# One operand of a VectorE product is read from PSUM instead of SBUF in a decode attention kernel

## The chip, the cores and the metric

The kernel runs on one core of one Trainium2 chip. The metric is device time in microseconds (us). Three runs of the kernel before took 1329.06, 1330.38 and 1332.26 us; the median is 1330.38 us. One further execution was recorded with the hardware profiler; every duration below is from it.

The engines are named as the profile names them: PE (TensorE, matrix products; PEld is its weight load), DVE (VectorE), ACT (ScalarE), POOL (GpSimd) and SP (SyncE, which here only starts transfers). SBUF is the working memory, PSUM the memory that PE writes its products to.

## What is computed

One decoding step of a transformer block with four sequences, one new token each:

```python
def _A_ref(x, k_cache, v_cache, wq, wo):          # B=4, Sq=1, D=512, H=32, Sk=4096, Dh=128
    q = (x @ wq).reshape(B, Sq, H, Dh).transpose(0, 2, 1, 3)
    scores = jnp.einsum("bhqd,bhkd->bhqk", q, k_cache) * (Dh ** -0.5)
    p = _softmax(scores, axis=-1)
    o = jnp.einsum("bhqk,bhkd->bhqd", p, v_cache)
    return o.transpose(0, 2, 1, 3).reshape(B, Sq, H * Dh) @ wo

mod = (_silu(c) @ w_mod).reshape(c.shape[0], 6, 1, -1)
sa, ca, ga, sb, cb, gb = (mod[:, i] for i in range(6))
h = _layernorm(x) * (1 + ca) + sa
x = x + ga * _A_ref(h, A_k_cache, A_v_cache, A_wq, A_wo)
h = _layernorm(x) * (1 + cb) + sb
x = x + gb * (_silu(h @ w1) @ w2)                 # F=1792
```

All arrays are float32. The two caches hold 4 x 32 x 4096 x 128 numbers each, 268 MB apiece, and every one of them is read once. The remaining inputs are weights of 1 to 8 MB.

## The kernel before

**Tiles.** The attention is cut into 32 tiles. A tile `n` is one sequence `b` and a group of four heads. Its keys are 8.39 MB (4 heads x 4096 x 128 x 4 bytes); its values are as many. A tile's keys lie in SBUF as 128 partitions by 128 rows of 128 numbers: partition `32*i + p` belongs to head `i` of the four.

**Buffers.** Three areas of 64 KB per partition, A, B and C. The keys alternate between B (even tiles) and A (odd tiles). There is one area, C, for the values.

**Order of the transfers.** All large transfers are started by SP from one queue, in the order of the program: the keys of tile n+1, then (after tile n) the values of tile n+1, then the keys of tile n+2, and so on. SP waits in front of a transfer until the area it overwrites has been read for the last time. So the values of n+1 are started when PE has finished the last product with the values of n; the keys of n+2, behind them in the queue, when tile n's keys have been read, which is earlier.

**One tile** (`tile`, then `values`):

- The keys are multiplied by the query in place: DVE takes the first 48 rows (its query operand lies in PSUM, banks 0 and 1, where `qload` puts it), POOL takes rows 48 to 128 in three instructions (48 to 80, 80 to 104, 104 to 128) with the query in SBUF.
- DVE sums each row (`scores`, `TENSOR_REDUCE sc<-k`): rows 0 to 48, then 48 to 80.
- For the first 80 rows DVE finds the maximum, ACT takes the exponentials, and `spread(0, 80)` writes `pz`: each exponential times a mask of four columns that is 1 for the partition's own head and 0 for the other three. This is 320 numbers per partition.
- DVE sums rows 80 to 104 and 104 to 128, and the same follows for these 48 rows: maximum, exponentials, `spread(80, 128)` with 192 numbers per partition.
- PE multiplies `pz` into the values (`pv`), first for rows 0 to 80 into bank 2, then for the rest into bank 3. The quotient by the sum of the exponentials and the merge of the two halves follow on DVE, ACT and PE.

The mask is `mask`, a tile of 128 x 4 numbers in SBUF, which DVE computes once at the start from the identity matrix.

```python
def spread(lo, hi):
    g0, g1 = lo // JJ, hi // JJ
    w = pz[:, g0:g1, :, :]
    tt("DVE", w, bc(ev[:, g0:g1, :], 2, HP), bc(bc(mask[:, :], 1, g1 - g0), 3, JJ))
```

`bc` repeats an operand along a dimension without copying it, so the mask's four columns are read again and again.

**Ahead of the loop** the modulation, the first layer norm and the queries are computed; PE uses bank 7 there for parts of the modulation and of the queries. **Behind the loop** the output weights `wot` (area B, four transfers) and the weights of the feed-forward part `w1t` (three transfers) and `w2t` (five transfers, both in area A) follow in SP's queue. PE projects the attention's output with `wot` into columns 0 to 127 of bank 7 (`project`), and the feed-forward part ends the program. The last tile's keys and values come in two transfers each (rows 0 to 80 and 80 to 128).

The order of the work on every engine is the order of the program. Waits are derived from which regions an operation reads and writes; in PSUM a region is a whole bank, within a quarter of the partitions.

Of the kernel before, what the change touches and what calls it, by code (L numbers as in the profile page):

```python
# [6 lines left out]
AF = mybir.ActivationFunctionType  # L7
# [177 lines left out]
def build(nc, x, kc, vc, wq, wo, w1, w2, c, wm, out):  # L185
    P = 128
# [3 lines left out]
    G = 4  # L190
    W = P // G
    HP = 4
# [4 lines left out]
    JJ = 4  # L197
# [13 lines left out]
    def sb(name, *shape, at=None):  # L211
        size = 4
        for s in shape:
            size *= s
        if at is None:
            at = base[0]
            base[0] += -(-size // 32) * 32
            assert base[0] <= nc.sbuf_usable_end, (name, base[0])
        return nc.alloc_sbuf_tensor_at(name, [P, *shape], F32, offset=at)
# [10 lines left out]
    bank = [nc.alloc_psum_tensor(f"ps{i}", [P, 512], F32) for i in range(8)]  # L230
    dsem = {}

    def dma(dst, src, tag, eng="SP"):
        if tag not in dsem:
            dsem[tag] = nc.alloc_semaphore("d_" + tag)
        s = dsem[tag]
        e = pl.eng[eng]
        return pl.op(eng, lambda: e.dma_start(dst, src), [], [dst], sem=s)  # L238

    def dve(f, reads, writes):  # L240
        return pl.op("DVE", f, reads, writes)

    def act(f, reads, writes):
        return pl.op("ACT", f, reads, writes)
# [14 lines left out]
    def tt(eng, o, a, b, op=ALU.mult):  # L259
        e, q = (V, dve) if eng == "DVE" else (GP, pool)  # L260
        return q(lambda: e.tensor_tensor(o, a, b, op=op), [a, b], [o])  # L261
# [10 lines left out]
    def actv(o, a, fn, scale=1.0, bias=None, accum=None):  # L272
        kw = {"scale": scale}
        reads, writes = [a], [o]
        if not isinstance(scale, float):
            reads.append(scale)
        if bias is not None:
            kw["bias"] = bias
            if not isinstance(bias, float):
                reads.append(bias)  # L280
        if accum is not None:
            kw["accum_out"] = accum
            writes.append(accum)
        return act(lambda: A.activation(o, a, fn, **kw), reads, writes)  # L284

    def bc(a, dim, n):
        a = a.unsqueeze(dim)
        shape = list(a.shape)
        shape[dim] = n
        return a.to_broadcast(shape)  # L290
# [4 lines left out]
    mask = sb("mask", G)  # L295
# [71 lines left out]
    def vload(n, *cuts):  # L367
        t, b = divmod(n, B)
        src = vc[b, HP * t : HP * (t + 1)].rearrange("h (p j) d -> (h p) j d", p=W)
        cuts = cuts or (0, NJ)  # L370
        for i, (lo, hi) in enumerate(zip(cuts, cuts[1:])):
            tag = "C" if len(cuts) == 2 else f"v{i}"
            dma(vt[:, lo:hi, :], src[:, lo:hi, :], tag)
# [83 lines left out]
    def qexpand(t):  # L457
        j, g = divmod(t, G)
        ps = bank[2 + t % 2]
        for i in range(HP):  # L460
            mm(
                ps[W * i : W * (i + 1), :], mask[:, g : g + 1].to_broadcast([P, W]),
                E[:, HP * j + i, :, :].rearrange("p b d -> p (b d)"), True, True,
            )
        actv(qw[:, t, :], ps[:, :], AF.Copy)
# [10 lines left out]
    for t in range(1, NT):  # L476
        qexpand(t)
    vload(0)
    for i in (2, 3):
        dve(lambda i=i: V.memset(bank[i][:, :], 0.0), [], [bank[i][:, :]])  # L480

    ev = ea.rearrange("p (g j) -> p g j", j=JJ)
# [7 lines left out]
    def spread(lo, hi):  # L490
        g0, g1 = lo // JJ, hi // JJ
        w = pz[:, g0:g1, :, :]
        tt("DVE", w, bc(ev[:, g0:g1, :], 2, HP), bc(bc(mask[:, :], 1, g1 - g0), 3, JJ))

    def ownmax(h, src, col):
        rm = sc[:, col : col + 1]
# [16 lines left out]
    def tile(n):  # L513
        t, b = divmod(n, B)
        k = kt[n % 2]
        tt("DVE", k[:, :ND, :], k[:, :ND, :], bc(bank[n % 2][:, :Dh], 1, ND))
        for lo, hi in zip(CUTS, CUTS[1:]):
            tt("POOL", k[:, lo:hi, :], k[:, lo:hi, :], bc(qview(n), 1, hi - lo))
        scores(n, (0, ND))
        scores(n, (ND, NA))  # L520
        ownmax(0, sc[:, :NA], NJ)
        actv(ea[:, :NA], sc[:, :NA], AF.Exp, bias=nm[:, 0:1], accum=rs[:, 0:1])
        spread(0, NA)
        for lo, hi in zip(CUTS[1:], CUTS[2:]):
            scores(n, (lo, hi))
        ownmax(1, sc[:, NA : NJ + 1], NJ + 1)
        actv(ea[:, NA:], sc[:, NA:NJ], AF.Exp, bias=nm[:, 1:2], accum=rs[:, 1:2])
        actv(X[:, 1:2], nm[:, 0:1], AF.Exp, scale=-1.0, bias=nm[:, 1:2])
        spread(NA, NJ)
        stt(X[:, 0:1], rs[:, 0:1], X[:, 1:2], rs[:, 1:2], ALU.mult, ALU.add)  # L530
        if n + 1 < N:
            qload(n + 1)
# [130 lines left out]
```

## Time and profile before

| | |
|---|---|
| median of three runs | 1330.38 us |
| profiled execution | 1325.98 us, of which the span from the first to the last instruction is 1324.6 us |
| DVE busy | 984.4 us, 74% of the span |
| POOL busy | 710.3 us, 54% |
| PE busy | 402.1 us, 30% |
| ACT busy | 83.8 us, 6% |
| read from HBM | 567.30 MB, 428 GB/s over the span |
| mean granted PE clock | 0.65 |

In the views of the profile a row of the timeline gives the start, the duration, the engine, the line of the code, the operation with its output and inputs, and in brackets how long the engine had stood idle before it and for what. A row of groups gives the busy time of all such instructions, the mean of one, and the idle time before them. A row of windows gives a stretch, its length, the busy time of each engine in it with the number of instructions, and at its end the granted PE clock, the share in which the 16 DMA engines were busy, and the rate of the transfers.

### The profile page before, as it was taken

How to read it: one execution, taken by the hardware profiler on the slowest of the kernel's cores; microseconds unless marked ns; L12 is line 12 of the kernel's file. 1: busy time of each engine (PE TensorE's matmuls, PEld its weight loads, DVE VectorE, ACT ScalarE, POOL GpSimd, SP SyncE). 2: the span in 40 equal slices, each digit the busy share in tenths (PEclk: the TensorE clock that was granted, in tenths of full speed). 3: DMA queues.
4: the chain of work that ended last, by engine and by line, in shares of the span. 5: the costliest groups of instructions: out<-in, count | busy, mean ns of one | idle time of the engine just before them, and what ended most of it. 6: DMA issues, size and time to landing. Idle time of an engine off the chain costs nothing.

```text
span 1324.6 us, 7211 instructions
## 1 busy us (share of the span) xinstructions
PE 402.1 (30%) x3032; PEld 122.9 (9%) x3032; DVE 984.4 (74%) x582; ACT 83.8 (6%) x289; POOL 710.3 (54%) x104
## 2 busy tenths in 40 slices
PE   2433212333311333322133332223333212333346
PEld 1100000000000000000000000000000000000014
DVE  1378877777887777788777778777778877777881
ACT  1200000000000000000000000000000000000001
POOL 0345665444666544566644456655445665444750
PEclk9766566666556666655666665566666566666577
DMA  9999999999999999999999999999999999999998
GB/s 412 442 414 439 440 424 434 418 440 422 438 437 432 429 432 426 440 433 434 433 426 435 436 434 430 433 428 431 434 424 438 433 424 436 432 431 430 424 423 344
DMA packets 12125, 567.78 MB, mean 429 GB/s; under 512 B 1292, under 2 KB 1340, under 8 KB 2108
## 3 DMA queue, kind: packets, MB, share of 16 engines
q1 hardware_dynamic: 12052, 567.29, 99.4%
q8 instruction: 24, 0.39, 0.1%
q14 instruction: 9, 0.07, 0.0%
q10 hardware_dynamic: 40, 0.02, 0.0%
HBM read 567.30 MB, written 0.01 MB: 428 GB/s over the span
## 4 chain that ended last, share of the span: by engine, by line
DMA 55%; DVE 36%; PE 6%; ACT 1%; issue 1%; SPq 1%; POOL 0%; another core or an unknown queue 0%
DMA k<-in_A_k_cache_dram 49%; DVE sc L270 22%; DVE k L261 8%; PE ps L252 6%; DVE pz L261 5%; DMA wot<-in_A_wo_dram 3%; DMA wqt<-in_A_wq_dram 3%; ACT sc L284 1%; DVE rt L499 1%; SPq L238 1%; DVE nm L269 0%; POOL E L261 0%; DVE hidT L402 0%; DVE hid L265 0%
## 5 line engine op out<-in xcount | busy, mean ns | idle before, releaser
L261 POOL TENSOR_TENSOR k<-k,qw 128x3072 f32<-128x3072 f32 (+1 forms) x96 | 705.8, 7380 | 521.6 <-DMA k<-in_A_k_cache_dram 521.6
L252 PE MATMUL ps<-v,pz 128*16 128x512 f32 x2048 | 312.1, 752 | 854.0 <-DVE pz L261 854.0
L270 DVE TENSOR_REDUCE sc<-k 128x24 f32<-128x3072 f32 (+2 forms) x128 | 559.3, 4409 | 1.1
L261 DVE TENSOR_TENSOR k<-k,ps 128x6144 f32<-128x6144 f32 x32 | 209.7, 6554 | 126.1 <-DMA k<-in_A_k_cache_dram 126.1
L252 PEld LDWEIGHTS ps<-v,pz 128*16 128x16 f32 x2048 | 57.7, 113 | 1051.3 <-DVE pz L261 887.4
L261 DVE TENSOR_TENSOR pz<-sc,mask 128x320 f32<-128x320 f32 x64 | 127.6, 1994 | 32.5 <-ACT sc L284 32.5
L284 ACT ACTIVATE sc<-sc,nm 128x80 f32<-128x80 f32 x64 | 22.3, 348 | 1015.4 <-DVE nm L269 1015.4
L265 DVE SCALAR_TENSOR_TENSOR o<-ps,fr,o 128x512 f32<-128x512 f32 x32 | 24.0, 750 | 52.7 <-PE ps L252 52.7
L252 PE MATMUL ps<-sel,o 128*128 128x4 f32 x256 | 33.8, 255 | 27.9 <-DVE o L265 27.9
L538 DVE RECIPROCAL fr<-ps 128x1 f32<-128x1 f32 x32 | 5.4, 168 | 42.5 <-PE ps L252 42.5
L252 PEld LDWEIGHTS ps<-sel,o 128*128 128x128 f32 x256 | 31.0, 191 | 59.9 <-DVE o L265 59.9
L261 POOL TENSOR_TENSOR E<-qs,sel 128x2048 f32<-128x2048 f32 x1 | 3.6, 3640 | 45.5 <-ACT qs L284 45.5
L284 ACT ACTIVATE o<-ps,fr 128x512 f32<-128x512 f32 x32 | 22.0, 687 | 60.8 <-DVE fr L265 60.8
L270 DVE TENSOR_REDUCE sc<-sc 128x1 f32<-128x80 f32 x64 | 14.1, 220 | 2.2
L499 DVE STREAM_TRANSPOSE rt<-sc 128x32 f32<-128x32 f32 x64 | 13.5, 212 | 2.2
L252 PE MATMUL ps<-wmt,csT 128*32 128x256 f32 (+1 forms) x64 | 8.3, 697 | 18.2 <-DMA wmt<-in_w_mod_dram 18.2
L284 ACT ACTIVATE oz<-ps 128x4 f32<-128x4 f32 (+2 forms) x40 | 7.4, 197 | 97.5 <-PE ps L252 97.5
L269 DVE TENSOR_REDUCE nm<-rt 128x1 f32<-128x32 f32 x64 | 11.9, 186 | 2.2
L261 DVE TENSOR_TENSOR E<-qs,sel 128x2048 f32<-128x2048 f32 x1 | 2.3, 2291 | 13.6 <-ACT qs L284 13.6
L252 PE MATMUL ps<-X,selp 128*128 128x2 f32 x64 | 12.3, 262 | 0.0
L252 PEld LDWEIGHTS ps<-X,selp 128*128 128x128 f32 x64 | 9.5, 188 | 27.3 <-DVE X L265 27.3
L284 ACT ACTIVATION_READ_ACCUMULATOR sc<-sc,nm 128x1 f32 x64 | 11.9, 186 | 0.0
(62 smaller groups left out, 121.2 us busy)
## 6 DMA issues: line engine op xcount, KB each, us to landing
wmt<-in_w_mod_dram SPq DMA_DIRECT2D x1, 6144.0 KB, 17.3
k<-in_A_k_cache_dram SPq DMA_DIRECT2D x1, 5120.0 KB, 35.9
v<-in_A_v_cache_dram SPq DMA_DIRECT2D x1, 5120.0 KB, 21.0
wot<-in_A_wo_dram SPq DMA_DIRECT2D x1, 4096.0 KB, 33.9
k<-in_A_k_cache_dram SPq DMA_DIRECT2D x1, 3072.0 KB, 42.8
v<-in_A_v_cache_dram SPq DMA_DIRECT2D x1, 3072.0 KB, 24.3
wot<-in_A_wo_dram SPq DMA_DIRECT2D x1, 2048.0 KB, 38.4
wot<-in_A_wo_dram SPq DMA_DIRECT2D x2, 1024.0 KB, 42.0
```

The costliest lines, as they stand in the source:

```text
L238: return pl.op(eng, lambda: e.dma_start(dst, src), [], [dst], sem=s)
L252: lambda: nc.tensor.matmul(o, lhsT, rhs, start=start, stop=stop, skip_group_check=True),
L261: return q(lambda: e.tensor_tensor(o, a, b, op=op), [a, b], [o])
L265: return dve(lambda: V.scalar_tensor_tensor(o, a, s, b, op0=op0, op1=op1), reads, [o])
L269: return dve(lambda: V.tensor_reduce(o, a, axis=AX.X, op=op, negate=True), [a], [o])
L270: return dve(lambda: V.tensor_reduce(o, a, axis=AX.X, op=op), [a], [o])
L284: return act(lambda: A.activation(o, a, fn, **kw), reads, writes)
L499: dve(lambda: V.transpose(rt[:, h, :], a), [rm], [rt[:, h, :]])
L538: dve(lambda: V.reciprocal(fr[:, 0:1], fps[:, 0:1]), [fps[:, 0:1]], [fr[:, 0:1]])
```

## The change

```diff
     for t in range(1, NT):
         qexpand(t)
     vload(0)
+    actv(bank[7][:, P : P + G], mask[:, :], AF.Copy)
     for i in (2, 3):
         dve(lambda i=i: V.memset(bank[i][:, :], 0.0), [], [bank[i][:, :]])
@@
     def spread(lo, hi):
         g0, g1 = lo // JJ, hi // JJ
         w = pz[:, g0:g1, :, :]
-        tt("DVE", w, bc(ev[:, g0:g1, :], 2, HP), bc(bc(mask[:, :], 1, g1 - g0), 3, JJ))
+        tt("DVE", w, bc(ev[:, g0:g1, :], 2, HP), bc(bc(bank[7][:, P : P + G], 1, g1 - g0), 3, JJ))
```

Ahead of the loop ACT copies the mask once into columns 128 to 131 of PSUM bank 7. Both spreads of every tile read it there. The numbers that are multiplied are the same. Nothing writes to bank 7 between this copy and `project`, behind the last tile, which writes its columns 0 to 127 when the last spread has been done.

ACT has one instruction more. It stands behind the last copy of an expanded query (`qw`), ahead of the load of the table for the exponentials and of the first tile's exponentials (`sc,rs<-sc,nm`):

```order
 L284 ACTIVATE ps<-qw 128x128
 L284 ACTIVATE qw<-ps 128x512 x7
+L284 ACTIVATE ps<-mask 128x4
 L284 ACT_TABLE_LOAD
 L284 ACTIVATE sc,rs<-sc,nm 128x80
```

Nothing behind it on ACT has another place. On DVE, in the first tile (`k_85` are its keys, `nm` the negative maximum, `pz` the spread exponentials), the changed kernel has:

```order
L269 TENSOR_REDUCE nm<-rt 128x1
L261 TENSOR_TENSOR pz<-sc,ps 128x320
L270 TENSOR_REDUCE sc<-k_85 128x24 x2
L270 TENSOR_REDUCE sc<-sc 128x1
L500 STREAM_TRANSPOSE rt<-sc 128x32
L269 TENSOR_REDUCE nm<-rt 128x1
L261 TENSOR_TENSOR pz<-sc,ps 128x192
```

The sequence is that of before; the two spreads name `ps` (PSUM) where they named `mask`. PE, POOL and SP have the same instructions in the same order.

## The prediction, made before the changed kernel had run

> **What bounds the kernel now.** The page comes first: the slices of the span, and the transfer queues.
>
> ```profile
> PE 402.1 (30%) x3032; PEld 122.9 (9%) x3032; DVE 984.4 (74%) x582; ACT 83.8 (6%) x289; POOL 710.3 (54%) x104
> DMA  9999999999999999999999999999999999999998
> GB/s 412 442 414 439 440 424 434 418 440 422 438 437 432 429 432 426 440 433 434 433 426 435 436 434 430 433 428 431 434 424 438 433 424 436 432 431 430 424 423 344
> q1 hardware_dynamic: 12052, 567.29, 99.4%
> DMA 55%; DVE 36%; PE 6%; ACT 1%; issue 1%; SPq 1%; POOL 0%; another core or an unknown queue 0%
> ```
>
> No compute engine is above 74%, while SP's one queue keeps the 16 DMA engines busy for 99.4% of the span and moves over 410 GB/s in every slice but the last. The last row is the chain of waits, and it seems to say something else: 36% of the span on DVE. So I look at one tile in the timeline, to see whether the transfers ever wait for DVE.
>
> ```profile
> 602.28 6.55 DVE L261 TENSOR_TENSOR k<-k,ps 128x6144 f32<-128x6144 f32 x1 [4.10 <-DMA k<-in_A_k_cache_dram]
> 602.33 22.05 POOL L261 TENSOR_TENSOR k<-k,qw 128x4096 f32<-128x4096 f32 x3 [16.65 <-DMA k<-in_A_k_cache_dram]
> 621.01 3.72 DVE L261 TENSOR_TENSOR pz<-sc,mask 128x320 f32<-128x320 f32 x1 [0.52 <-ACT sc L284]
> 624.65 6.60 DVE L270 TENSOR_REDUCE sc<-k 128x24 f32<-128x3072 f32 x2
> 624.78 6.19 PE L252 MATMUL ps<-v,pz 128*16 128x512 f32 x40 [25.49 <-DVE pz L261]
> 632.45 0.36 DVE L261 TENSOR_TENSOR pz<-sc,mask 128x192 f32<-128x192 f32 x1 [0.49 <-ACT sc L284]
> 636.13 0.33 SPq L238 DMA_DIRECT2D v<-in_A_v_cache_dram  x1
> 636.50 0.43 SPq L238 DMA_DIRECT2D k<-in_A_k_cache_dram  x1
> 640.98 6.55 DVE L261 TENSOR_TENSOR k<-k,ps 128x6144 f32<-128x6144 f32 x1 [4.09 <-DMA k<-in_A_k_cache_dram]
> ```
>
> Keys land at 602.28; 33.85 us later (636.13) PE is through with the values, and SP starts the next values and the next keys but one. The following keys, started a tile earlier, land only at 640.98. So when SP starts new transfers, 640.98 - 636.13 = 4.85 us of old ones are still under way. I call this the **cover**. The period is 640.98 - 602.28 = 38.70 us, and two transfers of 8.39 MB in it make 433.5 GB/s. The stretches by tile, and over the loop:
>
> ```profile
> 602.28:640.98 38.70, 10.45 (x74) 3.02 (x74) 30.48 (x17) 2.09 (x8) 22.05 (x3) 0.63 1.00 434
> 58.00:1224.60 1166.60, 330.83 (x2220) 92.03 (x2220) 914.36 (x510) 62.87 (x240) 661.66 (x90) 0.63 1.00 432
> ```
>
> The DMA share is 1.00 in both. **The transfers bound the loop.** DVE stands on the chain because SP starts the keys behind a wait for PE; a chain can't show that the transfer, once started, stands in line.
>
> **The change, part by part.** The groups with their shapes give the spread's price:
>
> ```profile
> L261 DVE TENSOR_TENSOR pz<-sc,mask 128x320 f32<-128x320 f32 x32 | 116.1, 3629 | 16.7 <-ACT sc L284 16.7
> L261 DVE TENSOR_TENSOR pz<-sc,mask 128x192 f32<-128x192 f32 x32 | 11.5, 359 | 15.8 <-ACT sc L284 15.8
> L261 DVE TENSOR_TENSOR E<-qs,sel 128x2048 f32<-128x2048 f32 x1 | 2.3, 2291 | 13.6 <-ACT qs L284 13.6
> L261 DVE TENSOR_TENSOR k<-k,ps 128x6144 f32<-128x6144 f32 x32 | 209.7, 6554 | 126.1 <-DMA k<-in_A_k_cache_dram 126.1
> ```
>
> The large spread takes ten times the small one, for 1.7 times the numbers. In the tile above POOL's three products end at 602.33 + 22.05 = 624.38, and the spread ends at 624.73, 0.35 us behind them. The small spread runs when POOL is idle. So DVE with two operands in SBUF stands still until POOL is done, whereas the keys' product, with one in PSUM, runs its 6554 ns beside POOL.
>
> *The spread's new time.* A line through the two rows that read SBUF alone and unhindered (192 numbers in 359 ns, 2048 in 2291) has 1.041 ns a number and 159 ns to begin with. It gives 492 ns for 320 numbers, and 6555 ns for 6144, where the row with a PSUM operand has 6554: PSUM costs nothing that shows. I take 0.49 us. Bounds: 0.36 us (the small spread) and 3.72 us (POOL still blocks it). [...]
>
> *What moves in a tile.* The large spread ends 3.72 - 0.49 = 3.23 us earlier, at 621.50. The next two sums take 6.60 us; the second starts near 624.8 and needs POOL's last product, done at 624.38, so it just finds it ready; if POOL were later, DVE would wait there. PE starts on `pz` at 621.6, is done with 40 products by 627.8, and the small spread is there at 632.45 + 0.36 - 3.23 = 629.58: PE still waits for DVE. So all that follows is 3.23 us earlier; SP starts the values at 632.90 instead of 636.13, and the cover becomes 8.08 us. DVE loses 32 x (3.63 - 0.49) = 100 us of busy time, 984 to 884, and its wait for the keys grows from 4.1 to 7.3 us a tile.
>
> *What the end gains:* nothing. A transfer started earlier stands longer in a line that is never empty. The same tile repeats, so loop: 0 of 1166.5 us.
>
> *ACT's copy of the mask*, once:
>
> ```profile
> L284 ACT ACTIVATE oz<-ps 128x4 f32<-128x4 f32 x32 | 5.7, 178 | 90.3 <-PE ps L252 90.3
> 55.29 1.28 ACT L284 ACT_TABLE_LOAD   x1
> 76.34 0.36 ACT L284 ACTIVATE sc<-sc,nm 128x80 f32<-128x80 f32 x1 [19.77 <-DVE nm L269]
> ```
>
> A copy of this size takes 178 ns (bounds 0 and the 0.60 us of a whole bank's copy). The table load behind it would end near 56.8 us, and ACT is next wanted at 76.34: the 19.77 us of idling hide it. Without them it would be 0.2 us, once. Both spreads wait for ACT's exponentials already, so no wait is added.
>
> *The last tile and the tail.*
>
> ```profile
> 1256.11 22.10 POOL L261 TENSOR_TENSOR k<-k,qw 128x4096 f32<-128x4096 f32 x3 [9.40 <-DMA k<-in_A_k_cache_dram]
> 1259.13 6.54 DVE L261 TENSOR_TENSOR k<-k,ps 128x6144 f32<-128x6144 f32 x1
> 1277.85 0.71 DVE L261 TENSOR_TENSOR pz<-sc,mask 128x320 f32<-128x320 f32 x1 [0.52 <-ACT sc L284]
> 1292.76 5.37 PE L252 MATMUL ps<-wot,oz 128*32 128x128 f32 x128 [0.93 <-DMA wot<-in_A_wo_dram]
> 1303.49 1.08 PE L252 MATMUL ps<-wot,oz 128*32 128x128 f32 x32 [1.51 <-DMA wot<-in_A_wo_dram]
> ```
>
> Here DVE comes to the keys late (POOL began at 1256.11, DVE at 1259.13), so it gains 3.0 us, and 0.2 us at the spread. But PE then waits for the weights at 1292.76 and again at 1303.49, both for DMA: the 3.2 us become waiting there. **Sum: 0 on 1325.98 us** (span 1324.6 and 1.4 around it). The profiled execution is 4.4 us below the median of the runs; a change of 0 leaves the median, **1330.4 us**.
>
> **The rivals.**
>
> *A: the cover was too small after all (faster).* The keys land 30 times between these rows:
>
> ```profile
> 58.10 6.56 DVE L261 TENSOR_TENSOR k<-k,ps 128x6144 f32<-128x6144 f32 x1 [2.16 <-DMA k<-in_A_k_cache_dram]
> 1224.60 6.55 DVE L261 TENSOR_TENSOR k<-k,ps 128x6144 f32<-128x6144 f32 x1 [4.10 <-DMA k<-in_A_k_cache_dram]
> ```
>
> That is 38.88 us a tile, 0.18 above the 38.70 of the tile shown; 30 x 0.18 = 5.5 us. If those were gaps because some of the 16 engines ran dry before SP's start, a cover of 8 us would close them: 1320.5, or 1324.9 by the runs. Against it stand the tiles in which PE was late:
>
> ```profile
> 870.52 0.33 SPq L238 DMA_DIRECT2D v<-in_A_v_cache_dram  x1
> 874.30 6.55 DVE L261 TENSOR_TENSOR k<-k,ps 128x6144 f32<-128x6144 f32 x1 [3.02 <-DMA k<-in_A_k_cache_dram]
> 912.86 6.55 DVE L261 TENSOR_TENSOR k<-k,ps 128x6144 f32<-128x6144 f32 x1 [3.95 <-DMA k<-in_A_k_cache_dram]
> ```
>
> The cover was 3.78 us there, and the next keys came 38.56 us later, no later than usual. Chance 0.10.
>
> *B: the DMA engines run further apart (slower).* A transfer has landed when the slowest of 16 engines has written its part. An engine that is ahead is now held at SP's start; with 3.23 us more in line it may get as far ahead again, and the slowest lags the mean by up to as much. It decides once engines differ by more than the old cover, 4.85 us, and costs once, not per tile, where the last `wot` lands: up to 3.2 us, 1329.2, or 1333.6 by the runs. For it: the intervals are not all equal (38.70, and 38.56 above). Against: every part of a transfer is of one size, and nothing in the rows shows engines apart. Chance 0.06.
>
> *C: the chain of waits is to be taken at its word (faster).* It passes DVE in every second tile: 16 x 3.23 = 52 us, 1274, or 1278 by the runs. Two tiles, 33.55 MB, would have to land in 77.40 - 3.23 = 74.17 us, 452 GB/s; the highest slice above is 442. [...] Chance 0.01.
>
> *D: the mask in PSUM doesn't free the spread.* It stays at 3.7 us; the time is the forecast's. Against it speaks the keys' product beside POOL. Chance 0.03.
>
> **How the numbers follow.** The forecast has 0.80. Its own range is the median with what three runs spread to either side and some more, 1327.9 to 1333.0. The range reaches towards A, down to where four fifths of the 5.5 us are gone (1326.0), and up to 1333.0; most of B and the far end of A are left out. A measurement of this kernel can tell about 0.2%, 2.7 us, from no change. Faster by more: A, C and 0.01 of the forecast's scatter, 0.12. Slower by more: B and 0.01 likewise, 0.07. Within: the rest with D, 0.81.
>
> **What would show it.** Right: the large spread near 0.5 us, DVE near 884 us busy, its wait for keys near 226 us in total (126.1 + 31 x 3.23), SP's start of the values 8 us before the keys land, keys still every 38.7 us, and in the tail longer waits of PE for `wot`. A is right if the intervals even out at 38.70; B if they, or the last `wot`, come later; D if the spread still ends with POOL. The forecast is wrong if the rate over the loop leaves 432 GB/s by more than 0.2% in either direction.

## The result, and the profile after

The changed kernel is faster: 1322.38 us (median of 4 runs, 1322.36 to 1322.80) against 1331.20 (4 runs, 1329.06 to 1332.26), a ratio of 0.9937 with a 95% interval of 0.9919 to 0.9954. In a second measurement of both (run g1 below) it was 1322.74 against 1328.46, ratio 0.9961 (0.9947 to 0.9976). That is 6 to 9 us, where the forecast was none. Two things stand out: the gain, and that the runs after lie within 0.4 us of each other where those of before spread over several. The profiled execution of before (1325.98) was faster than all four of its runs; the one after is 1322.36, with a span of 1321.0 us.

First the rows that the prediction named. The page of the changed kernel, engines, transfer queue and chain of waits:

```profile
PE 400.2 (30%) x3032; PEld 127.8 (10%) x3032; DVE 883.6 (67%) x582; ACT 83.9 (6%) x290; POOL 711.0 (54%) x104
q1 hardware_dynamic: 12052, 567.29, 99.5%
DMA 58%; DVE 34%; PE 6%; ACT 1%; issue 1%; SPq 0%; POOL 0%; another core or an unknown queue 0%
```

Its groups by shape (busy time in us, mean of one in ns, then the idle time ahead):

```profile
L261 DVE TENSOR_TENSOR k<-k,ps 128x6144 f32<-128x6144 f32 x32 | 209.7, 6554 | 218.9 <-DMA k<-in_A_k_cache_dram 218.9
L261 DVE TENSOR_TENSOR pz<-sc,ps 128x320 f32<-128x320 f32 x32 | 15.6, 487 | 16.7 <-ACT sc L284 16.7
L261 DVE TENSOR_TENSOR pz<-sc,ps 128x192 f32<-128x192 f32 x32 | 11.3, 354 | 15.8 <-ACT sc L284 15.8
```

The large spread takes 487 ns where it took 3629, the small one 354 where it took 359; VectorE is busy 883.6 us (forecast 884) and waits 218.9 us for keys (forecast 226). One tile in the timeline:

```profile
678.78 6.55 DVE L261 TENSOR_TENSOR k<-k,ps 128x6144 f32<-128x6144 f32 x1 [7.33 <-DMA k<-in_A_k_cache_dram]
678.82 22.08 POOL L261 TENSOR_TENSOR k<-k,qw 128x4096 f32<-128x4096 f32 x3 [16.62 <-DMA k<-in_A_k_cache_dram]
697.50 0.49 DVE L261 TENSOR_TENSOR pz<-sc,ps 128x320 f32<-128x320 f32 x1 [0.52 <-ACT sc L284]
698.24 6.32 PE L252 MATMUL ps<-v,pz 128*16 128x512 f32 x40 [25.68 <-DMA v<-in_A_v_cache_dram]
709.39 0.33 SPq L238 DMA_DIRECT2D v<-in_A_v_cache_dram  x1
717.48 6.55 DVE L261 TENSOR_TENSOR k<-k,ps 128x6144 f32<-128x6144 f32 x1 [7.33 <-DMA k<-in_A_k_cache_dram]
```

SP starts the next values 30.61 us after the keys land (33.85 before), and the cover is 717.48 - 709.39 = 8.09 us (4.85 before). The period of this tile is still 38.70 us. So every local step came out as forecast, and the time did not. The loop, from the first to the 31st landing of keys, in the windows of before and after:

```profile
58.10:1224.60 1166.50, 330.83 (x2220) 92.03 (x2220) 914.36 (x510) 62.87 (x240) 661.66 (x90) 0.63 1.00 432
```

```profile
57.90:1222.43 1164.53, 329.91 (x2220) 96.83 (x2220) 817.09 (x510) 62.87 (x240) 662.38 (x90) 0.63 1.00 433
```

It lost 2.0 us. The DMA share reads 1.00 in both; it does not tell them apart. The weights behind the loop, in the timelines of after:

```profile
1290.61 6.25 PE L252 MATMUL ps<-wot,oz 128*32 128x128 f32 x128 [3.15 <-DMA wot<-in_A_wo_dram]
1300.61 1.08 PE L252 MATMUL ps<-wot,oz 128*32 128x128 f32 x32 [0.67 <-DMA wot<-in_A_wo_dram]
1305.60 4.91 PE L252 MATMUL ps<-w1t,h2T 128*32 128x448 f32 x32 [1.38 <-DVE h2T L402]
```

The last products with `wot` start 2.88 us earlier than before (1303.49): 0.2 us of it from ahead of the loop, 2.0 from the loop, 0.7 from behind it. The other 0.7 us of the span's 3.6 lie behind that, where TensorE's products with `w1t` took 4.91 us against 6.10; in the other runs these took 4.7 to 6.1 us in kernels of either kind, so I count no gain there.

**What the share hides.** A transfer is spread over 16 DMA engines, and the trace records when each has landed its part (16 landings a transfer). From these records and from those of the packets (65,536 bytes each, nearly all 2.42 us long) I worked out, for the loop: how far apart the first and the last of the 16 parts of a transfer landed, early and late in the loop; how many packets took over 0.2 us longer than 2.42, apart from those within 1 us of a fetch of instructions (the page's queues named "instruction", 16 KB and 8 KB a packet); and for how long engines had no packet at all, added up over the engines (engine-us).

```
                    parts apart, us    long packets       engines idle,    loop,
                    first    last      without a fetch    engine-us        us
before              2.0      2.5        56                 9.8             1166.5
before (run i2)     1.7      2.9       112                27.1             1168.7
after               1.9      5.1         0                 0.0             1164.5
after (run g1)      2.1      5.2         0                 0.0             1164.5
```

Before, the parts of the keys never land further apart than 3.0 us in the first profile and 3.7 us in the second. After, the engines drift, step by step, to 5 us, and nothing holds them: no engine idles, and the 26 long packets that remain all lie beside a fetch. This is the picture from which the theories below start.

- **Theory 1, cover.** The 16 engines are out of step. One that leads has finished its share of the old transfers while the slowest has not. If SP's start comes too late for the leaders, they run dry and start anew. With more cover, a larger lead is possible before that happens.
- **Theory 2, port.** What costs is that VectorE stands still beside GpSimd, in itself (3629 ns for the large spread before, 487 after). "Port" is only a name here: the runs show the standstill.
- **Theory 3, placement.** The added instruction moves code or fetches.

### The profile page after: what moved, and what is told of

It is laid out like the page before. It is cut to its first block, busy times and chain, and to the rows that moved or that the text cites. A ratio compares the mean times of both kernels' runs of the same rounds, so it can differ in the third digit from the quotient of the medians.

```text
span 1321.0 us, 7212 instructions
## 1 busy us (share of the span) xinstructions
PE 400.2 (30%) x3032; PEld 127.8 (10%) x3032; DVE 883.6 (67%) x582; ACT 83.9 (6%) x290; POOL 711.0 (54%) x104
## 4 chain that ended last, share of the span: by engine, by line
DMA 58%; DVE 34%; PE 6%; ACT 1%; issue 1%; SPq 0%; POOL 0%; another core or an unknown queue 0%
DMA k<-in_A_k_cache_dram 53%; DVE sc L270 23%; DVE k L261 8%; PE ps L252 6%; DMA wqt<-in_A_wq_dram 3%; DMA w2t<-in_B_w_dram 2%; ACT sc L284 1%; DVE pz L261 1%; DVE rt L500 1%; DVE nm L269 1%; SPq L238 0%; POOL E L261 0%; DVE o L265 0%; ACT qs L284 0%
## 5 line engine op out<-in xcount | busy, mean ns | idle before, releaser
L261 DVE TENSOR_TENSOR k<-k,ps 128x6144 f32<-128x6144 f32 x32 | 209.7, 6554 | 218.9 <-DMA k<-in_A_k_cache_dram 218.9
L252 PEld LDWEIGHTS ps<-v,pz 128*16 128x16 f32 x2048 | 62.6, 113 | 1039.4 <-DVE pz L261 882.5
L261 DVE TENSOR_TENSOR pz<-sc,ps 128x320 f32<-128x320 f32 x64 | 26.9, 421 | 32.5 <-ACT sc L284 32.5
L252 PE MATMUL ps<-wqt,hT 128*32 128x512 f32 x64 | 9.9, 786 | 10.6 <-DMA wqt<-in_A_wq_dram 10.6
```

The source lines that it names most:

```text
L252: lambda: nc.tensor.matmul(o, lhsT, rhs, start=start, stop=stop, skip_group_check=True),
```

## The experiments

All runs are set beside runs of the kernel before on the same chip (medians 1328.80, 1328.46 and 1330.19 us in the three sets).

**e1: the copy alone.** ACT copies the mask to PSUM; the spreads read SBUF.

```diff
     vload(0)
+    actv(bank[7][:, P : P + G], mask[:, :], AF.Copy)
```

> ACT copies the mask to PSUM as in the change, but both spreads still read the mask in SBUF. Theory 1 (cover): the time depends on how long before the end of the old transfers SP starts new ones (the cover, 4.85 us before the change, 8.1 after it), because the 16 DMA engines are out of step and those ahead run dry; the spread stays at 3.7 us, the cover at 4.85, and the time at that of before, about 1331. [...] Theory 3 (placement): the extra instruction moves the code or its fetches; then about 1322.

1330.99 us (1328.26 to 1335.89), ratio 1.0019 (1.0003 to 1.0034). The copy brings nothing; theory 3 falls.

**e2, g2, g4, g3: the changed kernel, with its cover taken away again.** VectorE does a useless sum of R rows ahead of the large spread. It writes a scratch column that the loop does not use.

```diff
         actv(ea[:, :NA], sc[:, :NA], AF.Exp, bias=nm[:, 0:1], accum=rs[:, 0:1])
+        red(dm[:, :], k[:, :R, :].rearrange("p j d -> p (j d)"))
         spread(0, NA)
```

R = 27 (e2):

> The changed kernel with one more sum on VectorE in each tile, over 27 rows of keys (3456 numbers, 3.74 us by the rows of the sums), ahead of the large spread; 0.5 us of it lies in the wait for ScalarE, so all that follows is about 3.2 us later, and the cover is back at 4.85 us. [...] Theory 1 (cover): back to the time of before, 1329 to 1332. Theory 2 (port): the changed kernel's time, 1322.4. The 16 partial landings of a transfer: at most about 2.6 us apart by theory 1, growing to 5 by theory 2.

R = 15 (g2), R = 40 (g3), and the unchanged after (g1) beside them:

> The changed kernel itself, beside the other runs of this set, which vary its cover of 8.1 us. Theory 1 (cover): its runs lie within 1 us of each other near 1322.4, those of before spread over 1325 to 1335.

> The changed kernel with a sum over 15 rows of keys ahead of the large spread (2.14 us, of which 1.6 us delay what follows): cover about 6.5 us. Theory 1: an engine is held when it leads the slowest by more than the cover less the 2.3 us from SP's start to the first bytes, here 4.2 us, which the changed kernel's engines reach only near 970 us: 1322.5 to 1324, and the partial landings stay within 4.2 us of each other. A theory by which any delay of the chain costs in proportion gives half of the gain back: about 1326.

> The changed kernel with a sum over 40 rows ahead of the large spread (5.47 us, 4.95 of delay): cover about 3.15 us, 0.9 us over the 2.3 us to the first bytes. Theory 1: engines are held in nearly every tile, every stall of one engine is paid by all, and held engines start anew with longer packets: 1333 to 1345, and the partial landings within about 1 us. If only a dry queue on all engines counted, the time of before or below: the cover is still positive, 1322 to 1330.

R = 34 (g4), between the two:

> The changed kernel with a sum over 34 rows of keys ahead of the large spread (4.67 us, 4.15 of delay): cover about 3.95 us. The runs so far have 1348.9 at 3.15, 1326.7 at 4.85, 1322.8 at 6.5 and 1322.7 at 8.1. Theory 1: steep between 3.15 and 4.85, so 1332 to 1340.

With the covers read from the traces (median over the tiles):

```
run      cover, us    time, us (range)               loop, us          long packets    engines idle,    parts apart
                                                     of the profile    w/o a fetch     engine-us        at the end, us
g3       3.9          1348.90 (1343.05 to 1359.35)   1183.0            236             121.4            2.5
g4       4.4          1338.63 (1334.98 to 1340.93)   1177.6            212              52.7            4.4
before   4.9          1328.46 (1324.06 to 1331.75)   1166.5, 1168.7    56, 112          9.8, 27.1       2.5, 2.9
e2       5.1          1326.72 (1324.36 to 1334.21)   1166.9             40              17.0            2.4
g2       6.7          1322.76 (1322.41 to 1324.08)   1164.8             35               3.9            2.9
g1       8.1          1322.74 (1322.53 to 1323.25)   1164.5              0               0.0            5.2
```

The time follows the cover, steeply below 5 us; between 6.7 and 8.1 it no longer changes. Part of the time of g3 and g4 is not the loop's: the sum delays the last tile too, and the last product with `wot` starts 5.8 and 4.1 us later after the 31st keys than in g1 without waiting for a transfer. The loops alone follow the cover as well. The tile of e2, in its timeline, shows that the cover is all that was given back:

```profile
680.52 6.55 DVE L261 TENSOR_TENSOR k<-k,ps 128x6144 f32<-128x6144 f32 x1 [4.28 <-DMA k<-in_A_k_cache_dram]
698.64 3.74 DVE L270 TENSOR_REDUCE dm<-k 128x1 f32<-128x3456 f32 x1
702.30 0.48 DVE L261 TENSOR_TENSOR pz<-sc,ps 128x320 f32<-128x320 f32 x1
714.17 0.33 SPq L238 DMA_DIRECT2D v<-in_A_v_cache_dram  x1
719.22 6.55 DVE L261 TENSOR_TENSOR k<-k,ps 128x6144 f32<-128x6144 f32 x1 [4.29 <-DMA k<-in_A_k_cache_dram]
```

The spread runs unhindered in 0.48 us, only later, and SP's start is back at 719.22 - 714.17 = 5.05 us ahead of the landing. The runs scatter over 10 us again, and the median is 4 us above g1's. That is against theory 2, which had 1322.4. The median is also below the 1329 to 1332 of theory 1, which is so far right in direction but not in size: some two thirds of the gain are lost again, not all of it. My figures for g3 were low (1333 to 1345); that 5 us of cover with 16 engines "busy" is near an edge is what the runs show.

In g3 the cover is still above zero in every tile (1.73 us at the least). Its window over most of the loop, columns as above:

```profile
100.00:1241.00 1141.00, 320.34 (x2146) 89.05 (x2146) 940.38 (x522) 60.77 (x232) 636.47 (x87) 0.63 1.00 426
```

A loop that is 18.5 us longer than after's (1183.0 in all) shows the same 1.00; only the last column, the rate, tells: 426 GB/s against 433.

**e3 and e4: more cover with the blocked spread kept.** The values of each tile come in two transfers; e3 is before with this, e4 is after with it. (The edit has a second line, which skips preparing a loop for TensorE that neither kernel uses.)

```diff
-            vload(n + 1)
+            vload(n + 1, 0, NA, NJ)
```

> The kernel before, mask in SBUF, spread blocked for 3.4 us as ever; but the values of each tile come in two transfers (rows 0 to 80 and 80 to 128), as in the last tile before, so that SP starts the first when the products with the first 80 rows are done, some 4.5 us earlier; the cover is about 9.4 us. Theory 1 (cover): 1322 to 1323. Theory 2 (port) and 3: 1331. The 16 partial landings drift 5 us apart by theory 1.

> The changed kernel with the same split of the values: cover about 13 us. Theory 1: the engines' lead at the end of the changed kernel, 5.2 us, and some 2.3 us from SP's start to the first bytes, 7.5 in sum, are already below 8.1, so no more is gained: 1322 within 0.1%. If engines were still running dry with a cover of 8.1: down to 1318 to 1320. Theory 2: 1322.

e3: 1326.96 us (1324.94 to 1327.96), ratio 0.9986 (0.9974 to 0.9999); e4: 1326.68 (1324.70 to 1327.33), 0.9975 (0.9962 to 0.9987). Neither is the 1322 that theory 1 gave, but they are alike, and their traces say why. e3's groups and its start of transfers:

```profile
L261 DVE TENSOR_TENSOR pz<-sc,mask 128x320 f32<-128x320 f32 x32 | 115.8, 3620 | 16.7 <-ACT sc L284 16.7
```

```profile
709.36 4.72 SPq L238 DMA_DIRECT2D v<-in_A_v_cache_dram  x2
714.13 0.43 SPq L238 DMA_DIRECT2D k<-in_A_k_cache_dram  x1
718.63 6.56 DVE L261 TENSOR_TENSOR k<-k,ps 128x6144 f32<-128x6144 f32 x1 [4.12 <-DMA k<-in_A_k_cache_dram]
```

The spread takes 3.6 us, blocked as before, the first half of the values starts 9.27 us ahead of the keys' landing, and no engine idles, no packet is long without a fetch, the parts drift 5.2 us apart: the state of after, with the spread as before. The loops are equal too, 1166.8 us in e3 and 1166.9 in e4. **So, with a cover of over 9 us, the blocked spread in itself cost nothing.** The 2.3 us above after's 1164.5 are the price of one more transfer a tile: its quiet period is 38.78 us in place of 38.70, and 30 x 0.08 = 2.4. The times lie 4 us above g1's; the rest is behind the loop. There the last product with `wot` starts 81.0 us (e3) and 80.7 us (e4) after the 31st keys, 79.0 in g1, although these weights land 78.1 us after them in all three; the traces don't say what it waits for.

**i1: the cover without PSUM.** The kernel before, with one sum moved ahead of the spread, so that GpSimd is nearly done when the spread comes.

```diff
+        scores(n, CUTS[1:3])
         spread(0, NA)
-        for lo, hi in zip(CUTS[1:], CUTS[2:]):
-            scores(n, (lo, hi))
+        scores(n, CUTS[2:4])
```

> The kernel before, mask in SBUF, with one line moved: VectorE sums rows 80 to 104 ahead of the large spread instead of behind it, so that GpSimd is nearly done (its third product ends 22.1 us after the keys land, the spread then starts at about 22.0) and the spread is blocked for 0.1 us instead of 3.4. TensorE's first 40 products start 3.3 us later than in the changed kernel and become the last thing to end: cover about 6.5 us. Theory 1 (cover): the time of the changed kernel with a cover of 6.5, 1322.8 to 1324. If PSUM itself matters in some other way: 1328.

1322.64 us (1322.62 to 1323.99), ratio 0.9952 (0.9936 to 0.9969): the changed kernel's time, with the mask in SBUF, and a little under the range given. Its timeline:

```profile
679.09 6.55 DVE L261 TENSOR_TENSOR k<-k,ps 128x6144 f32<-128x6144 f32 x1 [5.71 <-DMA k<-in_A_k_cache_dram]
700.47 1.07 DVE L261 TENSOR_TENSOR pz<-sc,mask 128x320 f32<-128x320 f32 x1
710.75 0.33 SPq L238 DMA_DIRECT2D v<-in_A_v_cache_dram  x1
717.79 6.55 DVE L261 TENSOR_TENSOR k<-k,ps 128x6144 f32<-128x6144 f32 x1 [6.28 <-DMA k<-in_A_k_cache_dram]
```

The spread is blocked for 0.6 us, SP starts 7.04 us ahead (6.7 in the median). Its loop takes 1164.3 us, with 0.2 engine-us of idling. Two kernels that gain their cover by different means have the same time.

**h1 and h2: fewer fetches of instructions.** TensorE's program of the first 31 tiles is written as a loop (h1: after, h2: before).

```diff
-LOOP = False
+LOOP = True
```

> The changed kernel with TensorE's program of the first 31 tiles written as a loop (its own switch for it), so that TensorE's instructions of one tile are fetched once, or at least not as new code in each tile; the work is the same. In the changed kernel's trace all 26 transfer packets of the loop that took over 0.2 us longer than the rest lie beside a fetch of 8 or 16 KB of instructions. If these fetches set the engines out of step: fewer fetches, long packets gone, partial landings 2 us apart at the end as at the start, and the 3.5 us by which the loop exceeds 30 x 38.70 mostly gone: 1318 to 1320.5. If the drift has another source: 1322, with landings 5 us apart as before.

> The kernel before with TensorE's 31 tiles as a loop: cover 4.85 us as before, but without TensorE's fetches of instructions, which are 18 of the 26 in the loop. If these fetches are what sets the engines apart, so that those ahead run dry: the loss of 6 us against the changed kernel shrinks with them to about 2, 1324 to 1325.5. If the late tiles do it, in which TensorE's clock comes up late and the cover falls to 3.4 us: 1328, unchanged.

The transfer queues of h1, as the page lists them (packets, MB, share):

```profile
q8 instruction: 6, 0.10, 0.0%
q14 instruction: 9, 0.07, 0.0%
```

The first had 24 packets in before and after. h1 took 1322.70 us (1322.43 to 1322.92), no less than after: the 1318 to 1320.5 did not come. Its parts still end 5.6 us apart, now in four steps of 0.6 to 1.0 us, at the places of four 8 KB fetches of the other queue. At each of them the part that lands last falls further behind and the other 15 keep their distances. These steps make up 3.5 of the 3.6 us by which its loop (1164.6 us) exceeds 30 x 38.70. In the trace of after two of the steps come with a 16 KB fetch alone (0.93 us at 562.50, 0.49 at 1105.83), and yet the sum is the same; why, the runs don't show. h2 took 1323.85 us (1323.10 to 1324.93), ratio 0.9959 (0.9943 to 0.9975): with before's cover of 4.85 us and its blocked spread, and 4.5 us less than before itself beside it (i2 below, 1328.34). The times say that the fetches matter when the cover is small, and not when it is large. The traces don't settle it: that of h2 has one tile with a cover under 4 us where the two of before have three and four, and its loop of 1166.1 us is only 0.4 us below that of the first profile of before.

**i2: before once more**, for a second profile.

> The kernel before itself, for a second profile of it: the first was of an execution 2 to 4 us below the median of its runs. Theory 1: the more tiles with a late start of the transfers (cover under 4 us), the longer the loop; the loop between the first and the 31st landing of keys takes more than 1166.5 us.

1328.34 us (1324.26 to 1332.36), ratio 0.9988 (0.9970 to 1.0005). The profiled execution of it took 1328.43; its loop is 1168.7 us, 4.2 above after's, with twice the long packets of the first profile. Four of its tiles have a cover under 4 us, three in the first profile. In those three TensorE's last 16 products with the values took 3.23 to 3.48 us, at a granted clock of 0.53 to 0.57, where the tile at 602.28 has 1.91 us at 1.00. One tile more is too little to be the whole difference.

## Why the prediction was wrong

**Right, step by step:** the spread's time (0.49 us forecast, 487 ns), that PSUM costs nothing that shows (354 ns for the small spread, 359 from SBUF), the 3.23 us in each tile (3.24), the new cover (8.08, 8.09), VectorE's busy time, the hidden copy on ACT, and what blocked the spread: beside GpSimd's products it took 3629 ns with both operands in SBUF and 487 with one in PSUM. Rival D is out by the 487 ns, rival C by the 38.70 us that the tile kept.

**Wrong: the step "What the end gains: nothing. A transfer started earlier stands longer in a line that is never empty."** There are 16 lines, and some were empty for a time; with more cover the loop became 2.0 us shorter than in the first profile of before and 4.2 shorter than in the second. The support of the step was the DMA share of 1.00 and the period of 38.70 us. The share is a mean, in which 56 stretched packets don't show, and 10 engine-us of idling are 0.05% of 16 x 1166. The period that I took as the rule was the best of them; the mean was 38.88.

**Rival A was the right mechanism, with 0.10, and its bound by the runs (1324.9 us) was not low enough.** Three things went wrong with it.

- *Its size.* The 5.5 us came from one profile, of the best execution of four. The runs themselves spread from 1325.98 to 1332.26. The slack to be won was to be read there: in the profiles it is 2.0 and 4.2 us in the loop, in the medians 6 to 9 in all. Nor were the 5.5 us all gaps: after, the mean period is still 38.82 us, and 3.5 us in steps at the fetches remain. That 1320.5 and 1324.9 lay within 3 us of the results is luck.
- *Its test.* The late tile (cover 3.78, next landing 38.56 us on) seemed to clear it. But a landing is that of the slowest engine, which is the one that is not held. What a late start does is to take away the others' lead: the parts of the transfers around it land 3.0 us apart at 874.28 and 1.9 at 912.84. After, the parts stay 3.4 apart through those tiles. Nor is every late start so cheap: in i2 the keys behind one land 40.55 us after those before, as its timeline shows (cover 3.71).

```profile
1066.13 0.33 SPq L238 DMA_DIRECT2D v<-in_A_v_cache_dram  x1
1069.84 6.56 DVE L261 TENSOR_TENSOR k<-k,ps 128x6144 f32<-128x6144 f32 x1 [2.96 <-DMA k<-in_A_k_cache_dram]
1110.39 6.55 DVE L261 TENSOR_TENSOR k<-k,ps 128x6144 f32<-128x6144 f32 x1 [5.94 <-DMA k<-in_A_k_cache_dram]
```

- *Its threshold.* I compared the cover with zero. Leaders finish some 2 us ahead of the landing that I measure (parts apart, first column), and engines that have run dry take up their next packet mostly 1.0 to 4.0 us after SP's start (2.3 in the median over the two profiles of before and those of e2, g2, g3, g4 and h2). Together that is 3 to 6 us, not zero. The runs agree: at 4.9 and 5.1 us of cover time is lost, at 6.7 none.

**Rival B saw the drift and had its sign wrong.** The engines do run further apart, to 5.1 us. It costs nothing: the last `wot` landed 78.05 us after the 31st keys, 78.76 before. A reason that would fit, and that no run shows by itself: when each engine works through its own share, only the delays of the slowest count; when the leaders are held at each start, the delays of every engine may count.

What stays open: how exactly a held leader becomes lost time of the slowest. The runs show that long packets and idling appear with small cover and that the time goes with them. Added up, the idling and what the long packets without a fetch take beyond 2.42 us come, for each of the 16 engines, to 2.5 and 5.5 us in the two profiles of before, 11.3 in g4 and 15.8 in g3; their loops are 2.0, 4.2, 13.1 and 18.5 us longer than after's. That is the right size, but no proof. In h2 there are 87 long packets without a fetch and 23.2 engine-us of idling, more than in the first profile of before, 4.6 us for each engine, and yet its loop is only 1.5 us longer than after's; so this sum alone is not the measure. That a leader which has lost its lead is next to be the slowest, when a fetch falls on it, fits h2, but no run shows it by itself.

## What to carry to other kernels

When transfers bound a kernel, don't ask whether the queue is empty but by how much the next start precedes the end of the old transfers, and compare that with how far apart the DMA engines land; here 6.7 us were enough and 5.1 were not, though the share read 1.00. Work off the critical path is worth removing as long as it sets that start; here 3.24 us a tile of it brought 6 to 9 us in all. A spread between runs that the profile doesn't explain is itself a sign: here it was 3.2 us over the four runs before and 0.4 over the four after.

## What the runs showed of the hardware

- With two operands in SBUF, VectorE's product of 320 numbers stood still until GpSimd's product had ended (3629 ns); with one of them in PSUM it took 487 ns beside the same GpSimd work. The operand in PSUM, four columns read again and again, was no slower than in SBUF (354 ns against 359 for 192 numbers).
- Long packets stood beside fetches of instructions. In the loop after, beside each of the 26 fetches of 16 KB or 8 KB one packet of 65,536 bytes took 2.8 to 3.1 us instead of 2.42, and these were the only long packets.
- In the loop after, 1164.5 us long, the 16 parts of the keys landed 1.9 us apart at the first tiles and 5.1 at the last. The distance grew in steps at fetches (0.9 us at 562.50, 0.5 at 1105.83) and was kept between them: 3.4 us from 756.22 to 911.04.
- One transfer more a tile, of the same bytes, cost 0.08 us a tile in e3 (38.78 against 38.70 us), where no DMA engine idled in the loop.
